# ScalarE's table sets, the grouping of its wide passes, and VectorE's instruction forms in a fused attention and rational-MLP kernel

## The chip, the cores and the metric

The kernel runs on one core of one Trainium2 chip. The metric is the device time of one execution in microseconds (us). Five things work side by side on the core: TensorE (PE in the profile; PEld is its weight load), VectorE (DVE), ScalarE (ACT), GpSimd (POOL), and the queue of the SyncE engine (SP), which issues the DMAs.

## What is computed

There are 4 batches of 12,480 rows of 128 numbers. Two attention steps through 32 inducing points (`h = mab(I, x)`, then `mab(x, h)`) give a matrix with one row for each row of x. It then goes through a two-layer network whose activation is a quotient of polynomials:

```
s = scale * (q @ kv^T);  a = softmax(s);  out = a @ kv
h = x @ w_in                           # 49920 x 2048
P = a0 + a1*h + a2*h^2 + a3*h^3
Q = 1 + |b0|*|h| + |b1|*h^2
y = (P / (Q + 1e-6)) @ w_out
```

## The kernel before

The network is nearly all of the time. A **unit** is one block of 480 rows by two slices of 128 of the 2048 hidden features, so a block has 8 units, a batch 26 blocks, and the kernel 832 units. `fast_ticks` (line 927) writes one unit into every engine's program per turn of its loop, a **tick** t, and the program order is kept as written. For unit u a tick holds:

- PE: two products into PSUM (`hp<-at,st`) and, 17 ticks later, the four passes of the second product (`po<-l,w_out`). For even units a further pair adds a shift (`hp<-same,by`).
- For even units DVE takes the absolute value of `hp` into SBUF (`row<-hp`, tensor_scalar). For odd units ACT does it (`row<-hp,all`, the function Abs).
- One tick later DVE forms a product from that value and `hp` (`l<-row,all,hp`, scalar_tensor_tensor), which also frees the PSUM buffer, of which there are three.
- ACT turns the absolute value into the reciprocal of the denominator in two steps, in place: a logarithm (Ln, `row<-row`) and a sigmoid (`row<-row,all`).
- 15 ticks after the unit, DVE (odd t, `l<-l,all,row`, called k3 below) and POOL (`row<-l,all`, then `l<-row`) form the last products for two units together.

Two neighbouring units are a **pair**, and a pair's values lie in one **room** of a ring of 9 rooms in SBUF. ACT handles Ln and sigmoid for 10 units (5 pairs, a **group**) together, so that it must load its function tables twice per group. `wide` (line 985) says in which of the group's ten turns which pairs are handled: Ln for pairs 0 and 1 at turn 0, 2 and 3 at turn 2, 4 at turn 4; sigmoid for pair 0 at turn 5, 1 and 2 at turn 6, 3 and 4 at turn 8. Two pairs in neighbouring rooms are one instruction of 128 x 3840. Where the ring wraps between them, they are two of 128 x 1920. ACT's Abs comes at every even turn, ahead of that turn's wide work.

The attention for later blocks and batches is spread between the units (`side`). It gives ACT exponentials: `e` for the first attention step (`exp_rows`) and `a` for the second (`pass3`). `run_act(turn == TURNS)` (line 974) lets them run at turn 5 only, that is, after a group's last Ln and ahead of its first sigmoid. The kernel loads the table set that has both Ln and Exp once, at its start; every later table load stands where the compiler put it, ahead of the first instruction whose function the loaded set lacks.

VectorE also has small work once per batch: `thirds` (line 623) splits a 128 x 128 matrix `gl` into three bf16 parts, `pass1` (line 376) reduces a row maximum (`mt`) and scales it (`nm`), and `bounded` (line 639) folds a flag `over` into a 32 x 1 column.

Of the kernel before, what the change touches and what calls it, by code (L numbers as in the profile page):

```python
# [9 lines left out]
F32 = mybir.dt.float32  # L10
# [6 lines left out]
ALU = mybir.AluOpType  # L17
PSUM = bass.MemoryType.PSUM

P = 128  # L20
TP = 120
M = 32
C = 128
# [8 lines left out]
TURNS = 5  # L32
# [159 lines left out]
class Kernel:  # L192
# [46 lines left out]
    def cast(self, engine, out, in_):  # L239
        engine.tensor_scalar(out=out, in0=in_, scalar1=1.0, scalar2=0.0, op0=ALU.mult, op1=ALU.add)  # L240
# [44 lines left out]
    def setup(self):  # L285
        nc, cp = self.nc, self.cp
        self.ind = cp.tile([C, M], F32, name="ind")
        nc.sync.dma_start(out=self.ind, in_=self.ind_c)
        self.ident = cp.tile([P, P], F32, name="ident")
        make_identity(self.tc.nc, self.ident)  # L290
        self.ones = cp.tile([1, 4], F32, name="ones")
        nc.vector.memset(self.ones, 1.0)
        self.fold = cp.tile([P, M], F32, name="fold")
        for j in range(4):
            rows = slice(M * j, M * j + M)
            nc.vector.tensor_copy(out=self.fold[rows], in_=self.ident[rows, rows])
        self.many = cp.tile([M, 4], F32, name="many")
        nc.vector.memset(self.many, 1.0)
        self.w_max = cp.tile([C, 8], F32, name="w_max")
        self.w_in = cp.tile([C, self.F], F32, name="w_in")  # L300
        self.w_out = cp.tile([P, self.NF, C], F32, name="w_out")
# [74 lines left out]
    def pass1(self, b):  # L376

        nc, ap = self.nc, self.ap
        X = mybir.AxisListType.X
        e = ap.tile([P, self.NG, BT], F32, tag="e", name=f"e{b}")  # L380
        mxs = ap.tile([P, self.NG, 2], F32, tag="mxs", name=f"mxs{b}")
        nc.gpsimd.memset(mxs, -3.0e38)
        xs = Blocks([], self.wide_columns(b), ahead=False) if self.boot else self.cols.pop((b, "a"))
        for g in range(self.NG):
            nb = min(4, self.NB - 4 * g)
            yield from self.landed("a", b, g)
            yield "pe", 1.0
            pc = self.misc(f"pc{b}_{g}")
            for j in range(nb):
                nc.tensor.matmul(pc[M * j:M * j + M, 0:BT], self.ind, xs.take(), start=True, stop=True)  # L390
                xs.read()
            rows = slice(0, M * nb)
            for i in range(2):
                yield "v", 0.36
                c = slice(BT // 2 * i, BT // 2 * (i + 1))
                nc.vector.tensor_scalar(out=e[rows, g, c], in0=pc[rows, c], scalar1=1.0, scalar2=None, op0=ALU.mult, op1=ALU.max, accum_out=mxs[rows, g, i:i + 1])
            self.free()
        if self.boot:
            self.wide_rows(b)
        else:  # L400
            self.xs[b] = [self.x_rows(b, n) for n in range(4)]
        yield "v", 0.1
        mx = ap.tile([P, 1], F32, tag="mx", name=f"mx{b}")
        nc.vector.tensor_reduce(out=mx, in_=mxs.rearrange("p g i -> p (g i)"), axis=X, op=ALU.max)
        yield "pe", 0.2
        pm = self.misc(f"pm{b}")
        nc.tensor.transpose(out=pm[0:1, 0:P], in_=mx, identity=self.ident)
        yield "v", 0.3
        mt = ap.tile([1, 1, M], F32, tag="mt", name=f"mt{b}")
        nc.vector.tensor_reduce(out=mt[:, 0], in_=pm[0:1, 0:P].rearrange("o (j m) -> o m j", m=M), axis=X, op=ALU.max)  # L410
        self.free()
        nm = ap.tile([1, 4, M], F32, tag="H", name=f"nm{b}")
        nc.vector.tensor_scalar(out=nm, in0=mt.broadcast_to((1, 4, M)), scalar1=-1.0 / math.sqrt(C), scalar2=None, op0=ALU.mult)
        yield "pe", 0.2
        pb = self.misc(f"pb{b}")
        nc.tensor.matmul(pb[:, 0:4], nm.rearrange("o j m -> o (j m)"), self.ones, start=True, stop=True)
        yield "v", 0.1
        nmc = ap.tile([P, 1], F32, tag="nmc", name=f"nmc{b}")
        nc.vector.tensor_copy(out=nmc, in_=pb[:, 0:1])
        self.free()  # L420
        self.e[b] = e
        self.exps.append(lambda: self.exp_rows(b, e, nmc))
        self.flush()
# [199 lines left out]
    def thirds(self, b, g):  # L623

        V, lin = self.nc.vector, self.lin[b]
        top, rest = slice(0, 2 * M), slice(2 * M, 4 * M)
        parts = g[:, 3 * C:4 * C].bitcast(BF16).rearrange("p (i d) -> p i d", d=C)
        hi, mid = parts[:, 0], parts[:, 1]
        x, y, z = (g[:, C * i:C * i + C] for i in range(3))
        self.cast(V, hi, x)  # L630
        V.tensor_tensor(out=y, in0=x, in1=hi, op=ALU.subtract)
        self.cast(V, mid, y)
        V.tensor_tensor(out=z, in0=y, in1=mid, op=ALU.subtract)
        self.cast(V, lin[top, 0:C], x[top])
        self.cast(V, lin[rest, 0:C], y[rest])
        self.cast(V, lin[top, C:], z[top])
        V.memset(lin[rest, C:], 0.0)

    def bounded(self, b):

        nc, ap, p = self.nc, self.ap, self.params
        if b == 0:
            for j in range(4):
                for i, op in ((j, ALU.max), (4 + j, ALU.min)):
                    yield "v", 0.6
                    nc.vector.tensor_reduce(out=self.w_max[:, i:i + 1], in_=self.w_in[:, 512 * j:512 * j + 512], axis=mybir.AxisListType.X, op=op)
            yield "v", 0.3
            nc.vector.scalar_tensor_tensor(out=self.w_max[:, 0:4], in0=self.w_max[:, 4:8], scalar=-1.0, in1=self.w_max[:, 0:4], op0=ALU.mult, op1=ALU.max)
            nc.vector.tensor_reduce(out=self.w_max[:, 4:5], in_=self.w_max[:, 0:4], axis=mybir.AxisListType.X, op=ALU.max)
        yield "v", 0.15  # L650
        mag = ap.tile([C, M], F32, tag="H", name=f"mag{b}")
        nc.vector.scalar_tensor_tensor(out=mag, in0=self.HT[b][:, 0:M], scalar=-1.0, in1=self.HT[b][:, 0:M], op0=ALU.mult, op1=ALU.max)
        yield "pe", 0.2
        pm = self.misc(f"bound{b}")
        nc.tensor.matmul(pm[0:M, 0:4], mag, self.w_max[:, 4:8], start=True, stop=True)
        yield "v", 0.3
        r = slice(0, M)
        over = ap.tile([M, 1], F32, tag="over", name=f"over{b}")
        nc.vector.tensor_scalar(out=over, in0=pm[r, 0:1], scalar1=p.mag_kappa[r], scalar2=p.room[r], op0=ALU.mult, op1=ALU.is_gt)
        self.free()  # L660
        nc.vector.tensor_tensor(out=p.bad[r], in0=p.bad[r], in1=over, op=ALU.max)
        if b == self.B - 1:
            yield "pe", 0.2
            pn = self.misc("redone")
            nc.tensor.matmul(pn[0:1, 0:4], p.bad[r], self.many, start=True, stop=True)
            yield "v", 0.2
            nc.vector.tensor_scalar(out=p.redo[0:1], in0=pn[0:1, 0:1], scalar1=0.5, scalar2=None, op0=ALU.is_gt)
            self.free()
# [258 lines left out]
    def fast_ticks(self, units):  # L927
# [4 lines left out]
        V, A, p = self.nc.vector, self.nc.scalar, self.params  # L932
        n = len(units)
# [7 lines left out]
        for t in range(n + BEHIND + 3):  # L941
            u, last, d, done = at(t), at(t - 1), at(t - BEHIND), at(t - BEHIND - 2)
            group, turn = divmod(t - TURNS - 2, 2 * TURNS)
            wide = self.wide(units, group, turn) if group >= 0 else None
# [27 lines left out]
            if u and plain(u):  # L972
                self.moved(u)
            self.run_act(turn == TURNS)
            for w in wide or ():
                if turn < TURNS:
                    A.activation(w, w, AF.Ln, bias=LAM, scale=LAM / Z)
                else:
                    A.activation(w, w, AF.Sigmoid, bias=p.lnc, scale=-2.0)
# [4 lines left out]

    def wide(self, units, group, turn):

        first = {0: (0, 2), 2: (2, 2), 4: (4, 1), TURNS: (0, 1), TURNS + 1: (1, 2), TURNS + 3: (3, 2)}
        k, n = first.get(turn, (0, 0))
        pairs = units[2 * (TURNS * group + k):2 * (TURNS * group + k + n):2]
        rows = []  # L990
        for u in pairs:
            r = self.at_room(u.n)
            if rows and rows[-1][1] == r:
                rows[-1][1] = r + 1
            else:
                rows.append([r, r + 1])
        return [self.row[:, lo:hi] for lo, hi in rows]
# [170 lines left out]
```

## Time and profile before

| what | value |
|---|---|
| runs | 2332.75, 2334.54, 2338.04 us; median 2334.54 |
| the profiled execution | 2333.67 us, span 2331.9 us |
| PE busy | 2153.3 us, 92% |
| VectorE busy | 2152.5 us, 92% |
| ScalarE busy | 2139.8 us, 92% |
| GpSimd busy | 1479.3 us, 63% |
| ScalarE's table loads | 195, 250.2 us in all |
| mean granted TensorE clock | 0.964 |

A share of busy time is a mean over the whole span; the first 7% of it (weights, the first batch's attention) has little to do with the rest. The rows below therefore also show busy times stretch by stretch. Idle time is a stretch's length less the busy time.

### The profile page before, as it was taken

The page shows a single profiled execution, that of the slowest core. Times are in us where ns is not written, and L with a number is a line of the kernel's source. Part 1 is how long each engine was busy: PE and PEld are TensorE (multiplying, and loading weights), DVE is VectorE, ACT ScalarE, POOL GpSimd, SP SyncE. Part 2 cuts the span into 40 slices and gives each one's busy share as a digit, 9 for nine tenths or more (in the row PEclk, how much of TensorE's full clock was granted, in tenths as well). Part 3 has the DMA queues.
Part 4 walks back from the last instruction along what each step waited for, and adds up shares of the span by engine and source line. Part 5 has one row for each costly group of instructions (what it writes and reads, how often), then busy time and mean ns, then how long its engine had stood idle before and what let it go on. Part 6 is the DMA issues. An engine that isn't in the chain of part 4 may idle for free.

```text
span 2331.9 us, 23875 instructions
## 1 busy us (share of the span) xinstructions
PE 2153.3 (92%) x7744; PEld 976.1 (42%) x7744; DVE 2152.5 (92%) x2372; ACT 2139.8 (92%) x1256; POOL 1479.3 (63%) x1039
## 2 busy tenths in 40 slices
PE   4378998999899999998999999989999999999997
PEld 2133444444344444444444444434444444444443
DVE  2788998999999999999999899999999999999995
ACT  1087999999899999998999999989999999999995
POOL 0234666676666666667666666776766676676666
PEclk7588999999999999999999999999999999999999
DMA  9302220131122101321231031001101100000000
GB/s 244 91 2 84 89 73 21 48 81 43 47 89 91 55 16 43 81 64 36 88 91 56 14 85 47 26 13 56 49 24 34 38 18 28 19 18 20 14 17 19
DMA packets 117103, 120.89 MB, mean 52 GB/s; under 512 B 13289, under 2 KB 115561, under 8 KB 116969
## 3 DMA queue, kind: packets, MB, share of 16 engines
q1 hardware_dynamic: 116969, 119.28, 17.7%
q8 instruction: 63, 1.03, 0.2%
q14 instruction: 71, 0.58, 0.1%
HBM read 80.89 MB, written 25.56 MB: 46 GB/s over the span
## 4 chain that ended last, share of the span: by engine, by line
PE 35%; ACT 27%; DVE 17%; issue 14%; DMA 2%; POOL 2%; SPq 1%; ACTq 0%; DVEq 0%; POOLq 0%
PE po L176 23%; ACT row L176 23%; PE hp L176 9%; DVE l L176 8%; DVE row L176 5%; ACT L176 4%; SPq L176 1%; DMA row<-x_c 1%; POOL l L176 1%; PE ph L176 1%; PE pc L176 1%; POOL row L176 1%; DMA raw<-w_in 1%; DVE gl L176 1%; PE pd L176 1%
## 5 line engine op out<-in xcount | busy, mean ns | idle before, releaser
L176 PE MATMUL po<-l,w_out 128*128 128x480 f32 x3328 | 1565.6, 576 | 6.4 <-POOL l L176 3.7
L176 DVE SCALAR_TENSOR_TENSOR l<-row,all,hp 128x960 f32<-128x960 f32 x832 | 1002.5, 1205 | 47.3 <-ACT row L176 36.3
L176 POOL TENSOR_TENSOR l<-row 128x960 f32<-128x960 f32 x416 | 930.3, 2236 | 34.6
L176 POOL TENSOR_SCALAR row<-l,all 128x960 f32<-128x960 f32 x416 | 445.4, 1071 | 697.2 <-DVE l L176 597.4
L176 PEld LDWEIGHTS po<-l,w_out 128*128 128x128 f32 x3328 | 620.1, 191 | 407.8 <-issue 239.6
L176 ACT ACTIVATE row<-row,all 128x3840 f32<-128x3840 f32 (+1 forms) x269 | 741.6, 2764 | 1.0
L176 ACT ACTIVATE row<-row 128x3840 f32<-128x3840 f32 (+1 forms) x268 | 717.4, 2683 | 6.5 <-DVE l L176 5.3
L176 DVE SCALAR_TENSOR_TENSOR l<-l,all,row 128x960 f32<-128x960 f32 x416 | 534.1, 1285 | 2.9 <-ACT row L176 2.9
L176 PE MATMUL hp<-at,st 128*128 128x480 f16 x1664 | 478.8, 370 | 47.3 <-DVE l L176 36.1
L176 DVE TENSOR_SCALAR row<-hp 128x960 int32<-128x960 int32 x416 | 476.9, 1146 | 10.9 <-PE hp L176 10.2
L176 ACT ACTIVATE row<-hp,all 128x960 f32<-128x960 f32 x416 | 436.5, 1049 | 47.9 <-PE hp L176 42.2
L176 PEld LDWEIGHTS <-st 128*128 128x128 f16 x1872 | 182.1, 98 | 533.7 <-issue 513.3
L176 PE MATMUL hp<-same,by 96*128 96x480 f16 x832 | 240.0, 369 | 35.8 <-DVE row L176 29.1
L176 ACT ACT_TABLE_LOAD x195 | 250.2, 1283 | 4.0 <-PEq L1161 0.7
L176 PEld LDWEIGHTS <-by 96*128 96x128 f16 x832 | 82.0, 99 | 227.9 <-issue 201.1
L176 DVE COPY oT<-po 128x480 f32<-128x480 f32 x104 | 67.9, 653 | 47.4 <-PE po L176 46.9
L176 PE MATMUL po<-at,st 128*128 128x480 f16 x208 | 60.0, 370 | 2.9 <-DVE st L176 2.9
L176 ACT ACTIVATE a<-a 120x512 f32<-120x512 f32 (+2 forms) x21 | 14.9, 727 | 35.7 <-DVE a L176 35.6
L176 ACT ACTIVATE e<-e,nmc 128x960 f32<-128x960 f32 (+1 forms) x16 | 15.6, 993 | 31.9 <-DVE nmc L176 31.7
L176 DVE TENSOR_SCALAR_CACHE_REDUCE e<-pc 128x240 f32<-128x240 f32 (+1 forms) x56 | 20.8, 402 | 24.8 <-PE pc L176 24.8
L176 POOL TENSOR_TENSOR row<-row 128x384 f32<-128x384 f32 (+2 forms) x11 | 11.8, 1075 | 43.2 <-DVE row L176 36.9
L176 POOL TENSOR_TENSOR a<-a,asm 120x512 f32<-120x512 f32 (+1 forms) x27 | 36.8, 1363 | 1.7 <-PE bound L176 1.7
(119 smaller groups left out, 599.0 us busy)
## 6 DMA issues: line engine op xcount, KB each, us to landing
xTb<-x_c SPq DMA_DIRECT2D x104, 240.0 KB, 3.3
out<-oT SPq DMA_DIRECT2D x104, 240.0 KB, 2.0
xTa<-x_c SPq DMA_DIRECT2D x78, 240.0 KB, 3.2
x<-x_t SPq DMA_DIRECT2D x78, 240.0 KB, 4.1
at<-hl SPq DMA_DIRECT2D x416, 30.0 KB, 1.8
row<-x_t SPq DMA_DIRECT2D x8, 720.0 KB, 14.2
row<-x_c SPq DMA_DIRECT2D x5, 960.0 KB, 12.3
raw<-w_in SPq DMA_DIRECT2D x4, 480.0 KB, 11.3
```

The costliest lines, as they stand in the source:

```text
L176: ins = call(*args, **kw)
```

## The change

Four edits:

- At turn 0 of each group the kernel itself asks for the table set that has both Ln and Exp (`preload_act_table_set`), ahead of the Ln instructions.
- `wide` has two timetables for Ln and two for sigmoid, and takes the one whose twos of pairs don't lie across the end of the ring (`cut` is the number of pairs up to it). It also returns nothing behind the last group.
- In `thirds` and `bounded`, tensor_scalar and tensor_tensor become scalar_tensor_tensor (times 1.0, then the operation; a cast is x*1 max x).
- In `pass1` the scaling instruction `nm` goes: the reduction writes its result four times, and the factor moves into the constant `ones` of the product behind it.

```diff
-        nc.vector.memset(self.ones, 1.0)
+        nc.vector.memset(self.ones, -1.0 / math.sqrt(C))
...
-        mt = ap.tile([1, 1, M], F32, tag="mt", name=f"mt{b}")
-        nc.vector.tensor_reduce(out=mt[:, 0], in_=pm[0:1, 0:P].rearrange("o (j m) -> o m j", m=M), axis=X, op=ALU.max)
+        mt = ap.tile([1, 4, M], F32, tag="H", name=f"mt{b}")
+        nc.vector.tensor_reduce(out=mt, in_=pm[0:1, 0:P].rearrange("o (a j m) -> o a m j", a=1, m=M).broadcast_to((1, 4, M, 4)), axis=X, op=ALU.max)
         self.free()
-        nm = ap.tile([1, 4, M], F32, tag="H", name=f"nm{b}")
-        nc.vector.tensor_scalar(out=nm, in0=mt.broadcast_to((1, 4, M)), scalar1=-1.0 / math.sqrt(C), scalar2=None, op0=ALU.mult)
...
-        self.cast(V, hi, x)
-        V.tensor_tensor(out=y, in0=x, in1=hi, op=ALU.subtract)
...
+        def cast(out, in_):
+            V.scalar_tensor_tensor(out=out, in0=in_, scalar=1.0, in1=in_, op0=ALU.mult, op1=ALU.max)
+
+        cast(hi, x)
+        V.scalar_tensor_tensor(out=y, in0=x, scalar=1.0, in1=hi, op0=ALU.mult, op1=ALU.subtract)
...
-        nc.vector.tensor_tensor(out=p.bad[r], in0=p.bad[r], in1=over, op=ALU.max)
+        nc.vector.scalar_tensor_tensor(out=p.bad[r], in0=p.bad[r], scalar=1.0, in1=over, op0=ALU.mult, op1=ALU.max)
...
             self.run_act(turn == TURNS)
+            if turn == 0 and wide:
+                A.preload_act_table_set("natural_log_exp_and_others")
             for w in wide or ():
...
-        first = {0: (0, 2), 2: (2, 2), 4: (4, 1), TURNS: (0, 1), TURNS + 1: (1, 2), TURNS + 3: (3, 2)}
-        k, n = first.get(turn, (0, 0))
+        if 2 * TURNS * group >= len(units):
+            return []
+        cut = -units[2 * TURNS * group].n % self.rooms["u"]
+        logs = {0: (0, 1), 2: (1, 2), 4: (3, 2)} if cut in (1, 3) else {0: (0, 2), 2: (2, 2), 4: (4, 1)}
+        sigs = {0: (0, 2), 2: (2, 2), 4: (4, 1)} if cut in (2, 4) else {0: (0, 1), 1: (1, 2), 3: (3, 2)}
+        k, n = (logs if turn < TURNS else sigs).get(turn % TURNS, (0, 0))
```

How it moves instructions, at two places. The first is ScalarE in batch 0, from the table load of one group to the sigmoid of its first pair; `a_2` is an exponential of the second attention step. Before:

```order
L176 ACT_TABLE_LOAD
L176 ACTIVATE row<-row 128x3840
L176 ACTIVATE row<-hp_4_7_1271,all 128x960
L176 ACTIVATE row<-row 128x1920 x2
L176 ACTIVATE row<-hp_5_1_1296,all 128x960
L176 ACTIVATE row<-row 128x1920
L176 ACT_TABLE_LOAD
L176 ACTIVATE a_2_1140<-a_2_1140 120x512
L176 ACT_TABLE_LOAD
L176 ACTIVATE row<-row,all 128x1920
```

And ScalarE at the same place in the changed kernel:

```order
L176 ACT_TABLE_LOAD
L176 ACTIVATE row<-row 128x1920
L176 ACTIVATE row<-hp_4_7_1272,all 128x960
L176 ACTIVATE row<-row 128x3840
L176 ACTIVATE row<-hp_5_1_1296,all 128x960
L176 ACTIVATE row<-row 128x3840
L176 ACTIVATE a_2_1140<-a_2_1140 120x512
L176 ACT_TABLE_LOAD
L176 ACTIVATE row<-row,all 128x1920
```

The load between the last Ln and the exponential is gone, the two halves at the ring's end are one instruction, and the single pair now comes first instead of last. Over the whole fast path there are 26 table loads fewer (27 gone, one new at the first group), and of 37 places with two halves in a row one is left. The group that starts with the first sigmoid in the last row is moved in the same way where its cut is 2 or 4.

The second place is VectorE in batch 0, where `thirds` prepares batch 1's matrix. Before:

```order
L176 SCALAR_TENSOR_TENSOR gl_3652<-prep_3637,base 128x128
L176 TENSOR_SCALAR gl_3652<-gl_3652 128x128
L176 TENSOR_TENSOR gl_3652<-gl_3652 128x128
L176 TENSOR_SCALAR gl_3652<-gl_3652 128x128
L176 TENSOR_TENSOR gl_3652<-gl_3652 128x128
L176 TENSOR_SCALAR st_3375<-gl_3652 64x128 x3
```

And VectorE there in the changed kernel:

```order
L176 SCALAR_TENSOR_TENSOR gl_3658<-prep_3643,base 128x128
L176 SCALAR_TENSOR_TENSOR gl_3658<-gl_3658 128x128 x4
L176 SCALAR_TENSOR_TENSOR st_3380<-gl_3658 64x128 x3
```

The same seven steps stand at the same place; only their form changed. The instructions of GpSimd, of the DMA queue and of TensorE keep their order.

## Rows read from the trace of the kernel before

**Rows 1.** Busy us (instructions) by stretch: PE, PEld, DVE, ACT, POOL; clock, DMA

```profile
181.00:338.00 157.00, 147.81 (x508) 64.41 (x506) 150.47 (x179) 142.43 (x83) 95.04 (x65) 0.96 0.28 84
572.00:770.00 198.00, 187.27 (x629) 82.40 (x628) 195.53 (x221) 182.96 (x102) 132.02 (x90) 0.97 0.22 69
1043.00:1270.00 227.00, 219.61 (x754) 97.61 (x752) 225.52 (x255) 216.62 (x124) 154.95 (x105) 0.98 0.23 71
1510.00:1640.00 130.00, 122.65 (x384) 54.91 (x383) 127.85 (x131) 120.62 (x69) 92.70 (x60) 0.97 0.10 33
338.00:572.00 234.00, 224.67 (x918) 105.54 (x919) 216.38 (x219) 231.41 (x141) 155.13 (x118) 0.98 0.18 48
770.00:1043.00 273.00, 264.65 (x1064) 123.59 (x1063) 258.15 (x260) 272.29 (x166) 181.09 (x136) 0.99 0.18 51
1270.00:1510.00 240.00, 232.33 (x944) 108.84 (x944) 225.69 (x227) 238.71 (x144) 157.76 (x121) 0.99 0.17 45
1640.00:2290.00 650.00, 631.15 (x1991) 284.39 (x1990) 629.53 (x592) 648.39 (x365) 442.02 (x276) 1.00 0.08 25
```

**Rows 2.** Timeline around an exponential (start, duration in us, engine; idle before, releaser)

```profile
1299.88 1.80 ACT L176 ACTIVATE row<-row 128x1920 f32<-128x1920 f32 x1
...
1301.69 1.28 ACT L176 ACT_TABLE_LOAD   x1
...
1302.99 1.10 ACT L176 ACTIVATE e<-e,nmc 128x960 f32<-128x960 f32 x1
...
1306.34 1.90 ACT L176 ACTIVATE row<-row,all 128x1920 f32<-128x1920 f32 x1
...
1309.22 1.22 DVE L176 SCALAR_TENSOR_TENSOR l<-row,all,hp 128x960 f32<-128x960 f32 x1 [2.41 <-ACT row L176]
```

**Rows 3.** ScalarE's groups by shape: count, busy us, mean ns

```profile
L176 ACT ACT_TABLE_LOAD x195 | 250.2, 1283 | 4.0 <-PEq L1161 0.7
L176 ACT ACTIVATE row<-row 128x3840 f32<-128x3840 f32 x148 | 503.3, 3400 | 3.1 <-DVE l L176 2.1
```

**Rows 4.** Timeline of ScalarE: one wide sigmoid, one in halves, and the first Ln

```profile
670.82 3.48 ACT L176 ACTIVATE row<-row,all 128x3840 f32<-128x3840 f32 x1
...
675.15 3.67 ACT L176 ACTIVATE row<-row,all 128x1920 f32<-128x1920 f32 x2
...
130.64 3.40 ACT L176 ACTIVATE row<-row 128x3840 f32<-128x3840 f32 x1
```

**Rows 5.** Timeline of VectorE and GpSimd: k3 beside GpSimd's product, in batch 0

```profile
397.40 2.23 POOL L176 TENSOR_TENSOR l<-row 128x960 f32<-128x960 f32 x1
...
398.60 2.05 DVE L176 SCALAR_TENSOR_TENSOR l<-l,all,row 128x960 f32<-128x960 f32 x1
...
1297.47 1.21 DVE L176 SCALAR_TENSOR_TENSOR l<-l,all,row 128x960 f32<-128x960 f32 x1
```

**Rows 6.** Timeline of VectorE and GpSimd: the split of `gl` in batch 0

```profile
613.92 0.28 DVE L176 SCALAR_TENSOR_TENSOR gl<-prep,base 128x128 f32<-128x128 f32 x1
614.23 0.24 DVE L176 TENSOR_SCALAR gl<-gl 128x128 bf16<-128x128 f32 x1
614.48 2.23 POOL L176 TENSOR_TENSOR l<-row 128x960 f32<-128x960 f32 x1
614.51 2.35 DVE L176 TENSOR_TENSOR gl<-gl 128x128 f32<-128x128 f32 x1
```

**Rows 7.** Timeline of VectorE: `mt` and `nm`; below, a reduction of 512 elements, grouped

```profile
333.68 0.27 DVE L176 TENSOR_REDUCE mt<-pm 1x32 f32<-1x128 f32 x1
333.99 2.22 DVE L176 TENSOR_SCALAR nm<-mt 1x128 f32<-1x128 f32 x1
...
L176 DVE TENSOR_REDUCE amx<-ps 120x16 f32<-120x512 f32 x24 | 16.4, 685 | 1.9 <-PE ps L176 1.9
```

**Rows 8.** Timeline of ScalarE and VectorE: an Abs and the product that reads it

```profile
689.87 1.06 ACT L176 ACTIVATE row<-hp,all 128x960 f32<-128x960 f32 x1 [0.79 <-PE hp L176]
...
694.73 1.20 DVE L176 SCALAR_TENSOR_TENSOR l<-row,all,hp 128x960 f32<-128x960 f32 x1
```

More of the change, by code (lines that the diff above doesn't have):

```diff
@@ L408, in pass1 @@
         yield "v", 0.3
-        mt = ap.tile([1, 1, M], F32, tag="mt", name=f"mt{b}")
-        nc.vector.tensor_reduce(out=mt[:, 0], in_=pm[0:1, 0:P].rearrange("o (j m) -> o m j", m=M), axis=X, op=ALU.max)
+        mt = ap.tile([1, 4, M], F32, tag="H", name=f"mt{b}")
+        nc.vector.tensor_reduce(out=mt, in_=pm[0:1, 0:P].rearrange("o (a j m) -> o a m j", a=1, m=M).broadcast_to((1, 4, M, 4)), axis=X, op=ALU.max)
         self.free()
-        nm = ap.tile([1, 4, M], F32, tag="H", name=f"nm{b}")
-        nc.vector.tensor_scalar(out=nm, in0=mt.broadcast_to((1, 4, M)), scalar1=-1.0 / math.sqrt(C), scalar2=None, op0=ALU.mult)
         yield "pe", 0.2
         pb = self.misc(f"pb{b}")
-        nc.tensor.matmul(pb[:, 0:4], nm.rearrange("o j m -> o (j m)"), self.ones, start=True, stop=True)
+        nc.tensor.matmul(pb[:, 0:4], mt.rearrange("o j m -> o (j m)"), self.ones, start=True, stop=True)
         yield "v", 0.1
@@ L629, in thirds @@
         x, y, z = (g[:, C * i:C * i + C] for i in range(3))
-        self.cast(V, hi, x)
-        V.tensor_tensor(out=y, in0=x, in1=hi, op=ALU.subtract)
[L632 to L636, printed above, removed]
+        def cast(out, in_):
+            V.scalar_tensor_tensor(out=out, in0=in_, scalar=1.0, in1=in_, op0=ALU.mult, op1=ALU.max)
+        cast(hi, x)
+        V.scalar_tensor_tensor(out=y, in0=x, scalar=1.0, in1=hi, op0=ALU.mult, op1=ALU.subtract)
+        cast(mid, y)
+        V.scalar_tensor_tensor(out=z, in0=y, scalar=1.0, in1=mid, op0=ALU.mult, op1=ALU.subtract)
+        cast(lin[top, 0:C], x[top])
+        cast(lin[rest, 0:C], y[rest])
+        cast(lin[top, C:], z[top])
         V.memset(lin[rest, C:], 0.0)
```

## The prediction

> **What bounds the kernel now.** I read busy time by stretch first, because the page's 92% for each of three engines decides nothing. Rows of the view fall into two kinds [rows 1]. In the four stretches from 338, 770, 1270 and 1640 us, 1397 us in all, ScalarE is busy 231.4 + 272.3 + 238.7 + 648.4 = 1390.8 us, so it idles for 6 us, while VectorE idles for 67 us (1397 less 216.4 + 258.2 + 225.7 + 629.5). There ScalarE sets the pace. In the other four, 712 us in all, VectorE idles for 13 us and ScalarE for 49: there VectorE does. What a shorter ScalarE program is worth must be read from the first kind, and what a shorter VectorE program is worth from the second. TensorE idles for 44 us in the first kind, so it stands close behind both.
>
> Next I read the timeline where an exponential runs [rows 2]. The last Ln ends at 1301.68, a table load of 1.28 us follows at once, then two exponentials, a second load and, at 1306.34, the sigmoid, and behind that the next Abs. VectorE has waited 2.41 us for that Abs when it goes on at 1309.22. So the loads lie on the path there. The first of the two is the one that goes.
>
> **The change part by part.** The sum is made against the profiled execution, 2333.7 us; the median of the runs, 2334.5, is 0.8 above it.
>
> *Table loads.* The trace has 195 [rows 3]. The order of the changed kernel has 27 fewer and one new. A load costs its 1.283 us and, beyond that, an overlap: two neighbouring sigmoids of 1.90 us each [rows 2] are together 3.67 and not 3.80 [rows 4], so ACTIVATEs overlap by some 0.1 us, while a load starts only when the instruction ahead has ended, and the next only when the load has [rows 2]. So 1.38 us each. By their place in the trace, 17 of the 27 lie in the stretches that ScalarE bounds (5, 5, 4 and 3). 17 x 1.38 = 23.5 us, all of it on the path, because ScalarE has no idle time there and VectorE has 67 us to take the gain from.
>
> *Halves.* A wide sigmoid takes 3.48 us, one in two halves 3.67 [rows 4], so 0.19 us per place. Of the 37 places, 24 lie in those stretches: 4.6 us. Together with the loads, 28.1.
>
> *The same two edits where VectorE bounds.* Ten loads and eleven halves would be 10 x 1.38 + 11 x 0.19 = 15.9 us of ScalarE. VectorE covers them. The gain lies between 0 and VectorE's 12.6 us of idle time, and since that is only 1.8% of these stretches, against 4.8% in the others, I take 1.5.
>
> *The new load in the first group.* 1.4 us on ScalarE, which starts that group's first Ln at 130.64 us [rows 4] and is the late one there. Between 0 and 1.4; I take 1.4, a loss.
>
> *Does Ln cost the same from the shared set?* Until the first sigmoid, the kernel before still has the set loaded that it asked for at its start. Its first Ln, at 130.64 us, took 3.40 us [rows 4], as the mean of all [rows 3]. So nothing is lost there.
>
> *`nm` and `mt`.* The scaling goes. In the row shown it took 2.22 us behind a reduction of 0.27 [rows 7]; another of the four took 2.29, the other two 0.21. The reduction now reads 512 elements instead of 128; the nearest row, 512 elements per partition on 120 partitions, takes 0.685 [rows 7]. So two places go from 2.5 to 0.7 us and a third loses 0.2 (the fourth is in the start). Both long ones are at 334 and 760 us, where VectorE bounds: 3.7 - 0.2, a gain of 3.5.
>
> *The three-operand form.* What makes the small work long is not its length. The tensor_tensor on `gl` at 614.51 us lasts 2.35 us, to 616.86, just beyond the end (616.71) of a GpSimd product that began 0.03 us before it; a cast just ahead took 0.24 and a scalar_tensor_tensor that reads PSUM 0.28 [rows 6]. Eight instructions of `thirds` and `bounded` were held up in that way, by some 12 us in all. Does the new form escape? The trace has one of this form with both inputs in SBUF, k3. Started at 398.60 us inside a GpSimd product that ended at 399.63, it lasted 2.05 us, to 1.02 behind that end; free, it lasts 1.21 [rows 5]. It was held up too. I take the hold-ups to stay: 0. What is left is the cast, 0.28 against 0.24, seven per batch: a loss of about 1 us over four batches. The bounds are -12 (all escape) and +3 (the seven are also held up where they were not).
>
> The Trainium skill ("SBUF — State Buffer", section "Who interferes with whom") speaks against this edit: a VectorE instruction with two SBUF inputs shares a read interface with GpSimd instructions that read SBUF, and whichever comes second waits for the whole of the first. It puts tensor_tensor and every other form with two SBUF inputs on one footing. By that rule this edit is worth 0. By the one free row of 0.28 it would be worth the 12 us.
>
> *Sum.* -28.1 - 1.5 + 1.4 - 3.5 + 1.0 = -30.7, so 2333.7 - 30.7 = **2303**. Late next, once ScalarE is 28 us shorter, is VectorE: its 67 us of idle time in ScalarE's stretches fall to about 39.
>
> **The rivals.**
>
> *VectorE takes over sooner.* Its 67 us are not all slack: part is waiting for TensorE or for GpSimd, and k3 is held up more often as VectorE draws level. For it: the longest stretch that ScalarE bounds, of 650 us, holds only 20 us of VectorE's idle time [rows 1]. Against it: the wait of 2.41 us just behind an exponential [rows 2]. If half of the 28 is lost, the time is 2317.
>
> *The new form escapes GpSimd.* For it: the free 0.28 of a scalar_tensor_tensor [rows 6]. Against it: k3 [rows 5]. 12 us more, since nearly all of it lies where VectorE bounds: 2291.
>
> *A longer run between two Abs, and slower.* Where the cut is 1 to 4, the new timetables put two pairs in one instruction beside the change of tables: a Ln of 3.40 in place of 1.80, or a sigmoid of 3.48 in place of 1.90, between the Abs of turn 4 and that of turn 6. This run grows by 1.6 us in 37 groups. If each is a wait of VectorE, that is 59 us, and the time is 2333.7 + 59 - 30.7 = 2362. What decides is ScalarE's lead over VectorE. Where VectorE bounds, an Abs ended at 690.93 and was read at 694.73, a lead of 3.8 us [rows 8], which covers 1.6. Where ScalarE bounds, the lead is nothing [rows 2], but the other runs of that group become shorter by the same amount, and a ScalarE that never idles loses nothing by a different order. The rival wins if TensorE, held up with VectorE, can't keep ScalarE fed afterwards; with 44 us of idle time in 1397 it has little to make up with.
>
> *A change of tables costs more than the load's own bar.* Then each load gone is worth more. In the trace the load starts 0.01 us behind the Ln and the exponential 0.02 behind the load [rows 2], so I give it 1 in 100. With a further 1.4 us of ScalarE, about a load's own length, for each of the 17, the time would be 2303 - 24 = 2279. The Trainium skill ("ScalarE: Activation LUTs", section "What ACT_TABLE_LOAD costs") has such a price, 1283 ns and a drain of 1380 ns, 2.66 us in all; by it the loads would bring 45 us instead of 23.5. The trace shows the first figure and no drain.
>
> *The change doesn't do what it says.* The new order shows the loads gone, and the explicit load where the implicit one stood. Nothing is left of this but that something unseen eats the gain: 2 in 100.
>
> **How the numbers follow.** The forecast has 0.58, VectorE's taking over 0.22, the escape 0.12, the slower case 0.05, the drain 0.01, no effect 0.02. The forecast alone, with its bounds of 1.5 to 12.6 for ScalarE's work under VectorE, 0 to 1.4 for the new load and a few microseconds of shifted hold-ups, reaches from 2293 to 2313. The range has to take in most of the escape (2291) and of the take-over (2317): 2286 to 2321. About 0.2%, 4.7 us, can be told from no change. Faster by more than that are all cases but the slower one and no effect, and the slower one, met halfway, may come out even: 0.93 faster, 0.03 the same, 0.04 slower.
>
> **What the profile after would show.** Right: 169 table loads; no load between a Ln and an exponential; VectorE's wait behind it about 1 us instead of 2.4; ScalarE's busy time down by about 42 us (26 x 1.38 + 36 x 0.19), VectorE's idle time in ScalarE's stretches down to about 39 us; tensor instructions on `gl` that still last about 2 us beside a GpSimd product. Wrong: the `gl` steps all at 0.3 us (the escape); ScalarE idle for 20 us or more in the stretches it bounds now (take-over); VectorE waiting for Abs in groups whose cut is 1 to 4, by 1.6 us more than in the others, with ScalarE idle behind it (slower).

## The result and the profile after

The changed kernel takes 2312.16 us (median; 2310.33 to 2313.14), the kernel before, run beside it on the same chip, 2333.64. The ratio is 0.9904, with a 95% interval of 0.9887 to 0.9921. The profiled execution took 2313.14 us, with a span of 2311.3. So the change makes the kernel faster by about 21 us, where 31 were forecast. The time lies in the forecast range, and 9 us above the forecast.

The page of the changed kernel, its busy times and its groups (columns as in [rows 3]; the third part is the idle time just before the group and what ended most of it):

```profile
PE 2146.0 (93%) x7744; PEld 975.0 (42%) x7744; DVE 2147.9 (93%) x2368; ACT 2101.0 (91%) x1193; POOL 1483.0 (64%) x1039
...
L176 DVE SCALAR_TENSOR_TENSOR l<-row,all,hp 128x960 f32<-128x960 f32 x832 | 999.5, 1202 | 32.4 <-ACT row L176 23.7
...
L176 PE MATMUL hp<-at,st 128*128 128x480 f16 x1664 | 477.2, 369 | 42.8 <-DVE l L176 32.9
L176 ACT ACTIVATE row<-hp,all 128x960 f32<-128x960 f32 x416 | 436.7, 1050 | 62.2 <-PE hp L176 61.3
...
L176 ACT ACT_TABLE_LOAD x169 | 216.8, 1283 | 3.5 <-PEq L1168 0.7
```

Two of these groups in the kernel before:

```profile
L176 DVE SCALAR_TENSOR_TENSOR l<-row,all,hp 128x960 f32<-128x960 f32 x832 | 1002.5, 1205 | 47.3 <-ACT row L176 36.3
...
L176 ACT ACTIVATE row<-hp,all 128x960 f32<-128x960 f32 x416 | 436.5, 1049 | 47.9 <-PE hp L176 42.2
```

Table loads fell from the 195 of [rows 3] to 169, as forecast, at the same 1283 ns each. ScalarE is busy 38.8 us less than before (2139.8 less 2101.0). But the kernel gained only 20.6 us of span, so ScalarE now idles more. What it waits for is the fourth row: ahead of an Abs it waits 62.2 us in all, 61.3 of them for TensorE, against 47.9 and 42.2 before.

Where the time went is read stretch by stretch, as in [rows 1]. The eight stretches below hold the same instructions as those of [rows 1]: each boundary is moved by as much as the copy `oT<-po` of the nearest block of 8 units moved. The view of the changed kernel (busy us by stretch: PE, PEld, DVE, ACT, POOL; clock, DMA):

```profile
182.65:337.92 155.27, 147.57 (x506) 64.37 (x504) 148.75 (x178) 135.22 (x76) 95.07 (x65) 0.95 0.27 85
337.92:567.07 229.15, 223.35 (x919) 105.14 (x919) 217.04 (x219) 225.32 (x134) 155.27 (x118) 0.99 0.18 49
567.07:761.79 194.72, 185.50 (x629) 81.67 (x628) 193.36 (x220) 178.82 (x96) 131.34 (x90) 0.98 0.23 70
761.79:1030.16 268.37, 262.21 (x1064) 123.02 (x1063) 258.30 (x261) 266.17 (x157) 183.03 (x137) 1.00 0.19 52
1030.16:1257.62 227.46, 220.14 (x754) 97.73 (x752) 225.93 (x254) 214.16 (x117) 155.12 (x105) 0.98 0.23 70
1257.62:1492.06 234.44, 230.98 (x944) 108.33 (x944) 225.35 (x227) 231.62 (x136) 157.06 (x121) 1.00 0.17 46
1492.06:1621.80 129.74, 122.19 (x384) 54.91 (x383) 128.00 (x131) 120.19 (x66) 92.62 (x60) 0.97 0.10 33
1621.80:2268.51 646.71, 630.17 (x1991) 284.82 (x1990) 629.55 (x592) 642.10 (x351) 444.42 (x276) 0.99 0.08 25
```

The four stretches that ScalarE bounds (second, fourth, sixth, eighth) were 1397 us long and are 1378.7: a gain of 18.3. In them ScalarE is busy for 1365.2 us instead of 1390.8, and idles for 13.5 instead of 6.2. The other four were 712 us and are 707.2: a gain of 4.8. The part ahead of the first stretch grew by 1.65 us and the part behind the last by 0.9. That makes -18.3 - 4.8 + 1.65 + 0.9 = -20.6, the difference of the two spans.

The place of [rows 2] in the changed kernel. The timeline has ScalarE's last Ln, two exponentials without a load between, the one load that is left and the sigmoid, and VectorE's product behind the next Abs:

```profile
1283.27 3.40 ACT L176 ACTIVATE row<-row 128x3840 f32<-128x3840 f32 x1 [0.36 <-DVE l L176]
1286.58 1.08 ACT L176 ACTIVATE e<-e,nmc 128x960 f32<-128x960 f32 x1
1287.56 1.04 ACT L176 ACTIVATE a<-a 120x1024 f32<-120x1024 f32 x1
1288.62 1.28 ACT L176 ACT_TABLE_LOAD   x1
1289.92 1.90 ACT L176 ACTIVATE row<-row,all 128x1920 f32<-128x1920 f32 x1
...
1292.79 1.21 DVE L176 SCALAR_TENSOR_TENSOR l<-row,all,hp 128x960 f32<-128x960 f32 x1 [0.50 <-ACT row L176]
```

VectorE's wait here fell from the 2.41 us of [rows 2] to 0.50, although the last Ln is now the wide one. It is 0.13 in the kernel with the same loads and the old timetable (below).

### The profile page after: what moved, and what is told of

Same layout as the page of the kernel before. It is cut to its first block, busy times and chain, and to the rows that moved or that the text cites. A ratio compares the mean times of both kernels' runs of the same rounds, so it can differ in the third digit from the quotient of the medians.

```text
span 2311.3 us, 23789 instructions
## 1 busy us (share of the span) xinstructions
PE 2146.0 (93%) x7744; PEld 975.0 (42%) x7744; DVE 2147.9 (93%) x2368; ACT 2101.0 (91%) x1193; POOL 1483.0 (64%) x1039
## 4 chain that ended last, share of the span: by engine, by line
PE 47%; DVE 20%; ACT 16%; issue 12%; POOL 2%; DMA 2%; SPq 1%; DVEq 0%; POOLq 0%; ACTq 0%
PE po L176 31%; ACT row L176 13%; PE hp L176 12%; DVE l L176 10%; DVE row L176 6%; ACT L176 2%; SPq L176 1%; PE ph L176 1%; DMA row<-x_c 1%; POOL l L176 1%; PE pd L176 1%; PE pc L176 1%; POOL row L176 1%; DVE gl L176 1%; DVE oT L176 1%
## 5 line engine op out<-in xcount | busy, mean ns | idle before, releaser
L176 DVE SCALAR_TENSOR_TENSOR l<-row,all,hp 128x960 f32<-128x960 f32 x832 | 999.5, 1202 | 32.4 <-ACT row L176 23.7
L176 POOL TENSOR_SCALAR row<-l,all 128x960 f32<-128x960 f32 x416 | 448.1, 1077 | 673.8 <-DVE l L176 603.8
L176 ACT ACTIVATE row<-row,all 128x3840 f32<-128x3840 f32 (+1 forms) x250 | 738.1, 2953 | 1.0
L176 ACT ACTIVATE row<-row 128x3840 f32<-128x3840 f32 (+1 forms) x250 | 715.9, 2864 | 8.0 <-DVE l L176 6.8
L176 DVE SCALAR_TENSOR_TENSOR l<-l,all,row 128x960 f32<-128x960 f32 x416 | 533.3, 1283 | 4.6 <-ACT row L176 4.6
L176 PE MATMUL hp<-at,st 128*128 128x480 f16 x1664 | 477.2, 369 | 42.8 <-DVE l L176 32.9
L176 ACT ACTIVATE row<-hp,all 128x960 f32<-128x960 f32 x416 | 436.7, 1050 | 62.2 <-PE hp L176 61.3
L176 ACT ACT_TABLE_LOAD x169 | 216.8, 1283 | 3.5 <-PEq L1168 0.7
L176 DVE TENSOR_SCALAR_CACHE_REDUCE e<-pc 128x240 f32<-128x240 f32 (+1 forms) x56 | 20.6, 397 | 24.4 <-PE pc L176 24.4
L176 POOL TENSOR_TENSOR row<-row 128x384 f32<-128x384 f32 (+2 forms) x11 | 11.9, 1085 | 42.8 <-DVE row L176 35.3
```

What stands on the lines that cost most here:

```text
L176: ins = call(*args, **kw)
```

## The experiments

The four edits were taken one by one first. My theory was the prediction's: the loads carry the gain, halves add a little, the three-operand form nothing. The rival after the result was that the new timetables of `wide`, and not some overlap of the gains, took away what is missing. Every kernel ran beside the kernel before on the same chip. The traces of two kernels agree block by block wherever nothing changed: of the 103 blocks of two kernels below that differ in the three-operand form alone, 94 are equal to 0.02 us. So I also give a difference "by blocks": the time from the first to the last copy `oT<-po`. It leaves out the kernel's start, since the first copy comes between 179.2 and 183.8 us in the twelve traces. It is taken from one execution of each kernel, so it has no spread of its own. By blocks the change gains 22.0 us.

**The table loads alone.**

```diff
             self.run_act(turn == TURNS)
+            if turn == 0 and wide:
+                A.preload_act_table_set("natural_log_exp_and_others")
```

> Only the explicit table load is kept; the timetables, the small VectorE work and the scaling are those of the kernel before. Theory A (the new timetables give back what they save): the 26 loads alone bring nearly all that is left of the change once the scaling is taken off, 18 to 24 us. Rival B (VectorE takes over sooner, as the prediction's rival says, and the timetables are worth their 0.19 us per place): the loads bring 11 to 15 us. By the prediction's own sum: 17 x 1.38 + 1.5 - 1.4 = 23.6 us.

Measured: 2310.05 us (2308.37 to 2313.58), ratio 0.9906 [0.9891, 0.9922]; 24.0 us gained by blocks. This one edit gives all that the whole change gives, and by blocks 2 us more.

**The timetables alone.** `wide` as in the changed kernel, all else as before.

```diff
-        first = {0: (0, 2), 2: (2, 2), 4: (4, 1), TURNS: (0, 1), TURNS + 1: (1, 2), TURNS + 3: (3, 2)}
...
+        logs = {0: (0, 1), 2: (1, 2), 4: (3, 2)} if cut in (1, 3) else {0: (0, 2), 2: (2, 2), 4: (4, 1)}
+        sigs = {0: (0, 2), 2: (2, 2), 4: (4, 1)} if cut in (2, 4) else {0: (0, 1), 1: (1, 2), 3: (3, 2)}
```

> Only the grouping of wide passes is changed. Theory A: even or slower, 0 to +5 us: in groups whose cut is 1 to 4 VectorE waits about 2.5 us for the Abs behind the longer run, TensorE waits with it and is slow afterwards, and ScalarE then idles 0.6 to 1.4 us. Rival B: 4 to 5 us faster (24 places x 0.19 us), with no more idle time of ScalarE.

Measured: 2338.79 us (2335.21 to 2344.17, 10 runs), ratio 1.0024 [1.0014, 1.0035]; 6.6 us lost by blocks. So this edit makes the kernel slower, by a little more than the 0 to 5 us expected. Its group of VectorE products:

```profile
L176 DVE SCALAR_TENSOR_TENSOR l<-row,all,hp 128x960 f32<-128x960 f32 x832 | 1000.1, 1202 | 57.3 <-ACT row L176 47.8 <-PE hp L176 9.0
```

VectorE waits 57.3 us ahead of this product, against 47.3 in the kernel before (36.3 of it for ScalarE). With the boundaries moved as above, the four stretches that VectorE bounds are 5.4 us longer and the four that ScalarE bounds 0.8. In the first four VectorE had not waited for ScalarE ahead of this product at all; now it waits some 5.3 us there. So the lead of 3.8 us at one place [rows 8] did not cover 1.6 at every place.

**`mt` and `nm` alone.** The edit of `pass1` and of `ones`, as in the diff of the change.

> Only the scaling instruction and the reduction ahead of it are changed. From the two blocks of the trace that became shorter around it (1.9 and 3.6 us): 5 to 6 us faster, about 0.2%. By the prediction's sum: 3.5 us. If those two blocks became shorter through the loads instead: under 1 us.

Measured: 2330.53 us, ratio 0.9991 [0.9982, 1.0001]; 3.2 us gained by blocks. By the times alone this can't be told from nothing, and the 5 to 6 us that I had expected did not come; the prediction's 3.5 is nearer. The trace shows the edit: the reduction that stands in place of both instructions takes 0.67 us in each of the four batches.

```profile
L176 DVE TENSOR_REDUCE mt<-pm x4: 671/672/679, 31.0 to 1225.8; 1x128 f32<-1x512 f32 x4
```

**The three-operand form alone.** The edits of `thirds` and `bounded`.

> Only the form of the instructions in thirds and bounded is changed. If the new form is held up by GpSimd as the old one is: within 1.5 us of the kernel before, and single steps on gl that last 2 us. If it escapes: 9 to 12 us faster, every step on gl at 0.3 us.

Measured: 2334.1 us, ratio 1.0004 [0.9996, 1.0013]; 0.26 us lost by blocks. The eight casts and eight subtractions in the view of the tile `gl` (shortest, median and longest, in ns):

```profile
L176 DVE SCALAR_TENSOR_TENSOR gl<-gl x16: 279/535/2290, 176.5 to 1541.0; 128x128 bf16<-128x128 f32 x8, 128x128 f32<-128x128 f32 x8
```

The longest still lasts 2.29 us: it starts at 614.08, 0.09 us behind the start of a GpSimd product, and ends 0.15 us behind that product's end. The new form is held up beside GpSimd as the old one was.

**Loads and `pass1` together**, with the old timetable and the old forms.

> The explicit load and the shorter scaling, with the timetables and the forms of the kernel before. Theory A (the four edits add up, and the timetables are a loss): 22.9 + 2.4 = 25 us below the kernel before, some 2307 to 2309 us, faster than the changed kernel and than the loads alone. Rival (the changed kernel's loss is not the timetables but the edits hiding each other): 2310 to 2313, no better than the loads alone.

Measured: 2305.69 us (2303.31 to 2308.55), ratio 0.9885 [0.987, 0.99]; 29.1 us gained by blocks, 7.1 more than by the whole change. A part of the change does better than the change.

**The sigmoids' timetable, and the logarithms', each on top of those two.** In each only one of the two lines above was put in.

> As the first of these four, with the new timetable for the sigmoid alone (groups whose cut is 2 or 4). Theory A (the long run between two Abs is the loss, worst where an exponential falls into it): 1 to 4 us slower than the first of these four, VectorE waiting some 2.5 us behind the load in these groups. Rival (the loss comes from the Ln timetable): level with it, or 1 us faster.

> The loads and the pass1 edit (2305.7 us measured) plus the new Ln timetable alone (cut 1 and 3). Theory (a longer run between two Abs holds up TensorE wherever an exponential or ScalarE-bound stretch follows): a loss of 2 to 4 us against 2305.7, 2307.5 to 2309.5, in the trace as block losses of 0.4 to 1.1 us near 360, 805 to 870, 1285, 1700 and 1820 us, with VectorE's idle time up by as much and TensorE's too, and nothing in the stretches that VectorE bounds. Rival (halves saved count where ScalarE bounds, as forecast): a gain of 2 to 3 us, 2303. Rival (the remaining loss of the changed kernel comes from the three-operand form): no change here, 2305 to 2306.5.

Measured: 2307.43 us (2303.35 to 2315.0) and 2307.12 (2305.43 to 2312.49), against 2305.69 for the two edits alone. By the times neither can be told from it. By blocks they lose 1.9 and 1.6 us, at places: the sigmoids' in the last batch (+1.6 and +1.1 us in two neighbouring blocks, 1.8 of it given back in the two after), the logarithms' near 360, 801 and 822 us (+0.4, +0.7, +1.0). In the stretches that VectorE bounds the logarithms' lose 0.55 us in one block. The sigmoids' lose 0.8 us in one block there and gain 1.8 in another, at 1077 us, where the flag's product in `bounded` happened to miss GpSimd: it took 0.15 us, against 2.23 with the two edits alone. Without that gain they would have lost 3.7. For the logarithms I had expected 2 to 4 us; they cost a little less.

**The changed kernel with the old timetable.**

> The changed kernel with the old timetable of the wide passes: loads, pass1 edit and three-operand form. Theory (the form costs about 0.3 us in each of three later batches and the timetable alone explains the rest): 2305.5 to 2307.5, that is 5 to 6 us faster than the changed kernel's 2312.2. Rival (the form matters beside the loads, since VectorE is nearer to bounding): 2308 or more.

Measured: 2305.68 us (2303.44 to 2310.16), ratio 0.9891 [0.9875, 0.9908]. The medians are 6.5 us below the changed kernel's, as expected, though the two intervals overlap. By blocks the difference is 6.6 us, and 0.5 from loads and `pass1` alone, of which 0.28 and 0.30 stand in the blocks where batches 1 and 2 split `gl`. So the new timetable takes away some 6.6 us, more than its two halves one by one (3.5, or 5.4 without the gain at 1077 us). The four stretches that ScalarE bounds, in this kernel:

```profile
334.58:563.28 228.70, 223.35 (x919) 104.99 (x919) 217.11 (x219) 226.74 (x138) 155.45 (x119) 0.99 0.18 49
...
757.96:1024.66 266.70, 262.37 (x1064) 123.03 (x1063) 258.75 (x261) 265.73 (x161) 183.09 (x137) 1.00 0.19 52
...
1252.10:1486.23 234.13, 230.98 (x944) 108.34 (x944) 225.41 (x227) 232.62 (x141) 157.15 (x121) 1.00 0.17 46
...
1615.54:2259.79 644.25, 629.17 (x1991) 283.72 (x1990) 629.56 (x592) 642.74 (x362) 444.52 (x276) 1.00 0.08 25
```

They last 1373.8 us, with 1367.8 of ScalarE: 6.0 idle, as much as before. With the new timetable ScalarE has 2.6 us less to do in them (1365.2) and idles 7.5 us more (13.5), so they are 4.9 us longer. In the first three, which hold 2.4 of the 4.9, TensorE's granted clock is the same with both timetables (0.99, 1.00, 1.00). With the old timetable the groups of waits are shorter too:

```profile
L176 DVE SCALAR_TENSOR_TENSOR l<-row,all,hp 128x960 f32<-128x960 f32 x832 | 999.8, 1202 | 26.4 <-ACT row L176 18.7 <-PE hp L176 6.9
L176 PE MATMUL hp<-at,st 128*128 128x480 f16 x1664 | 477.2, 369 | 36.8 <-DVE l L176 26.9 <-DMA at<-hl 5.5 <-POOL st L176 1.5
L176 ACT ACTIVATE row<-hp,all 128x960 f32<-128x960 f32 x416 | 436.5, 1049 | 54.8 <-PE hp L176 47.2 <-POOL l L176 7.0
```

**How one place loses.** In the last batch a group begins its sigmoids with two pairs in the changed kernel and with one in the kernel with the old timetable. First the changed kernel's timeline (ScalarE from the load on, VectorE's product, TensorE), then its busy times (as in [rows 1]) from 2050.0 and 2055.7 us:

```profile
2048.71 1.28 ACT L176 ACT_TABLE_LOAD   x1
2050.00 3.50 ACT L176 ACTIVATE row<-row,all 128x3840 f32<-128x3840 f32 x1
2053.41 1.05 ACT L176 ACTIVATE row<-hp,all 128x960 f32<-128x960 f32 x1
...
2061.20 1.06 ACT L176 ACTIVATE row<-hp,all 128x960 f32<-128x960 f32 x1 [0.63 <-PE hp L176]
...
2054.49 1.21 DVE L176 SCALAR_TENSOR_TENSOR l<-row,all,hp 128x960 f32<-128x960 f32 x1 [2.58 <-ACT row L176]
...
2055.75 0.56 PE L176 MATMUL hp<-at,st 128*128 128x480 f16 x2 [2.68 <-DVE l L176]
2056.32 4.38 PE L176 MATMUL po<-l,w_out 128*128 128x480 f32 x6
```

```profile
2050.00:2055.70 5.70, 3.07 (x11) 1.19 (x10) 3.12 (x4) 5.70 (x3) 3.12 (x2) 1.00 0.01 3
2055.70:2061.00 5.30, 5.25 (x11) 2.09 (x11) 5.30 (x6) 4.87 (x3) 3.30 (x2) 0.68 0.12 46
```

And the same place with the old timetable, timeline and busy times:

```profile
2042.25 1.90 ACT L176 ACTIVATE row<-row,all 128x1920 f32<-128x1920 f32 x1
2044.06 1.04 ACT L176 ACTIVATE row<-hp,all 128x960 f32<-128x960 f32 x1
...
2045.13 1.22 DVE L176 SCALAR_TENSOR_TENSOR l<-row,all,hp 128x960 f32<-128x960 f32 x1 [0.98 <-ACT row L176]
...
2046.40 0.57 PE L176 MATMUL hp<-at,st 128*128 128x480 f16 x2 [1.08 <-DVE l L176]
2046.96 2.68 PE L176 MATMUL po<-l,w_out 128*128 128x480 f32 x6
```

```profile
2046.30:2051.50 5.20, 5.10 (x15) 2.30 (x15) 5.20 (x7) 5.20 (x4) 3.21 (x2) 1.00 0.12 47
```

Behind the load stands a sigmoid of 3.50 us instead of 1.90. VectorE waits 2.58 us for the Abs instead of 0.98: the 1.6 us of the prediction's slower rival. TensorE waits 2.68 instead of 1.08. After that wait the granted clock of the next 5.3 us is 0.68, a mean between the levels 1.2 and 2.4 GHz, and six passes of the second product take 4.38 us; with the old timetable the clock stays at 1.00 and the same six take 2.68. With TensorE late by a further 1.7 us, ScalarE then waits 0.63 us for its next `hp`.

The wait by itself did not bring the clock down. The kernel with the timetables alone has the same wait at the same place (TensorE's timeline, then the busy times behind it):

```profile
2082.88 0.57 PE L176 MATMUL hp<-at,st 128*128 128x480 f16 x2 [2.68 <-DVE l L176]
2083.45 2.68 PE L176 MATMUL po<-l,w_out 128*128 128x480 f32 x6
```

```profile
2082.90:2088.20 5.30, 5.30 (x16) 2.38 (x16) 5.30 (x6) 5.30 (x4) 3.31 (x2) 1.00 0.13 46
```

There the clock stays at 1.00, the six passes take 2.68 us, and ScalarE does not wait for the `hp` behind them. Over the four blocks from this place on, the new timetable costs 0.6 us in the kernel where the clock fell (+1.6, +1.1, -1.2, -0.8) and gains 0.6 in the one where it did not (+1.6, -0.3, -1.3, -0.6). By the difference the slower clock cost about 1.2 us here. Why it fell in one kernel and not in the other stays open.

In the changed kernel VectorE has such a wait (2.47, 2.58, 2.59 us) at 1929, 2054 and 2153 us, where the kernel with the old timetable has 0.87, 0.98 and 0.97. The slower clock follows the last two. Behind the first, TensorE waits only 1.18 us and its clock stays at 1.00, and the block is 1.4 us longer all the same. In its other groups no such wait is longer than 1.28 us, but for one of 3.02 in the first group, which both kernels have. ScalarE's 0.63 us behind each of the two slow places is 1.3 of the 7.5 us that it idles more. The rest lies elsewhere, in waits for TensorE or VectorE that no run ties one by one to a longer instruction.

**The small work with its operands in PSUM.** If operands in SBUF are what exposes `gl`, then keeping the matrix and its remainders in the PSUM tile `prep` should end the hold-ups, in the old two-operand form. The subtractions then have one input in SBUF and the casts none. The step ahead of them writes `prep` too, and `prep` is given back only behind them. In the kernel before, the steps take (view of the tile `gl`):

```profile
L176 DVE TENSOR_SCALAR gl<-gl x8: 218/733/1150, 177.2 to 1539.8; 128x128 bf16<-128x128 f32 x8
L176 DVE TENSOR_TENSOR gl<-gl x8: 291/452/2345, 177.4 to 1540.9; 128x128 f32<-128x128 f32 x8
```

Not only the subtractions were held up: four of the casts, which have one input in SBUF, lasted 1.04 to 1.15 us beside a GpSimd instruction, and so did `nm`, with one input, for 2.22 [rows 7]. The edit:

```diff
-        x, y, z = (g[:, C * i:C * i + C] for i in range(3))
+        x, y, z = (pr[:, C * i:C * i + C] for i in range(3))
...
-        over = ap.tile([M, 1], F32, tag="over", name=f"over{b}")
+        over = pm[r, 4:5]
```

> The kernel before, but thirds keeps its matrix and both remainders in PSUM, so that no instruction on them has two inputs in SBUF, and bounded does the same with its flag. Theory A (the hold-up comes from the second SBUF input, whatever the form): every step lasts 0.2 to 0.4 us, TensorE's idle time at the three places falls from about 5 us each, and the kernel is 8 to 15 us faster. Rival (the small steps are slow for another reason, or VectorE's stall is covered there): steps of 2 us remain, or the time is within 2 us of the kernel before.

Measured: 2326.81 us (2318.58 to 2328.7, 8 runs), ratio 0.9967 [0.9955, 0.9978]. The steps, in the view of the tile `prep`:

```profile
L176 DVE TENSOR_SCALAR gl<-prep x8: 291/292/292, 174.7 to 1542.7; 128x128 bf16<-128x128 f32 x8
L176 DVE TENSOR_TENSOR prep<-prep,gl x8: 299/299/300, 175.1 to 1543.0; 128x128 f32<-128x128 f32 x8
```

None lasts longer than 0.30 us, where the same work took up to 2.35 [rows 6], and six of each eight ran beside a GpSimd instruction. The gain is 5.7 us, below the 8 to 15 expected.

**Loads, `pass1` and PSUM operands together.**

> The explicit load, the shorter scaling and the small work in PSUM together. If the gains add: 25 us and what the run above brings, 2292 to 2300 us, faster than every other version. If they hide each other: 2303 to 2308.

Measured: 2292.39 us (2291.29 to 2294.0), ratio 0.9826 [0.9813, 0.984]. It beats the kernel before by 40 us and the changed kernel by 20. On top of loads and `pass1` the PSUM operands bring 13.3 us. A part of that again goes through TensorE's clock. With loads and `pass1` only, TensorE's timeline behind the split of batch 1, and the busy times around it:

```profile
613.72 0.96 PE L176 MATMUL hp<-same,by 96*128 96x480 f16 x2 [4.52 <-DVE row L176]
```

```profile
609.00:613.50 4.50, 0.20 (x1) 0.00 (x0) 4.32 (x8) 4.37 (x3) 2.23 (x2) 0.82 0.00 0
613.50:618.00 4.50, 4.12 (x8) 1.55 (x8) 4.50 (x7) 0.00 (x0) 1.23 (x2) 0.50 0.38 116
```

With PSUM operands TensorE waits 2.63 us there, and the 5 us after it have a mean clock of 0.68, not 0.50:

```profile
604.10 0.96 PE L176 MATMUL hp<-at,st 128*128 128x480 f16 x2 [2.63 <-DVE l L176]
```

```profile
604.00:609.00 5.00, 4.91 (x13) 2.08 (x13) 4.97 (x8) 4.41 (x3) 3.68 (x4) 0.68 0.00 0
```

Behind the split of batch 2 the wait is 2.63 us as well (at 1079.80), and there the 5 us after it have a clock of 1.00.

Why the same edit brought 5.7 us alone and 13.3 beside the other two is answered in part. By blocks (5.1 and 13.2 us) two blocks differ by 8.1 us together; the other differences cancel. The block at 1226 us is 5.3 us longer with the edit alone and unchanged beside the other two; the one at 443 us is 4.1 and 1.3 us longer. In the first, with the edit alone, stands an `nm` that is now held up, where it took 0.21 us in the kernel before; the edit of `pass1` removes it:

```profile
1239.37 2.28 DVE L176 TENSOR_SCALAR nm<-mt 1x128 f32<-1x128 f32 x1
```

The second stays open. Alone, the edit's runs spread over 10 us.

## Why the prediction was right in part, point by point

| term | forecast, us | measured, us |
|---|---|---|
| loads, where ScalarE bounds | -23.5 | -23.2 (four stretches, old timetable, `pass1` with them; -22.4 for the loads alone) |
| halves and the new order there | -4.6 | +4.9 (1378.7 less 1373.8) |
| the other four stretches: ScalarE's work, `nm`, form | -1.5 - 3.5 + 1.0 = -4.0 | -4.8 |
| start (the new load) | +1.4 | +1.65, not told from its spread |
| the end, behind the last stretch | 0 | +0.9 |
| sum | -30.7 | -20.6 |

- **Loads: right.** The edit alone gives 4.3, 6.4, 5.9 and 5.8 us in the four stretches, 22.4 in all for 17 loads: 1.32 us each, against 1.38 taken. It gives 1.5 in the other four, as taken. The row of -23.2 is 1397 less the 1373.8 us of the changed kernel with the old timetable. That a drain comes on top of each load, the Trainium skill's 2.66 us ("ScalarE: Activation LUTs", section "What ACT_TABLE_LOAD costs"), would by an estimate from that figure have shown as about 45 us in these stretches; it is not there.
- **VectorE's cover: right.** In the stretches that VectorE bounds, ScalarE's busy time falls by 14.2 us in the changed kernel (662.6 to 648.4), and most of it becomes idle time. VectorE's idle time in ScalarE's stretches fell to 48.4 us, where 39 were forecast, and to 42.9 with the old timetable. So the rival that VectorE takes over sooner is not what happened.
- **`nm` and `mt`: right.** A gain of 3.5 was forecast; the edit alone gained 3.2 by blocks, and 5.1 on top of the loads (29.1 less 24.0).
- **The form: right.** 1.0 us of loss was forecast, 0.26 by blocks measured for the edit alone, and no hold-up went. The rule of the Trainium skill ("SBUF — State Buffer", section "Who interferes with whom") gave 0 for it, and the trace agrees: 2.28 us is the longest `gl` step in the changed kernel, 2.29 with this edit alone. The remedy that the rule points to, one input that is not in SBUF, took every subtraction to 0.30. Of the casts the prediction read only the free one of 0.24 [rows 6]; four of the eight lasted over 1 us in the same trace.
- **Halves: wrong, and this is the step that failed.** A gain of 4.6 was forecast and a loss of 4.9 measured. The size was off: the 0.19 us per place is a sigmoid's. By the groups' busy time a sigmoid's place saved 0.18 us (741.6 to 738.1 for 19) and a logarithm's 0.09 (717.5 to 715.9 for 18); in these stretches ScalarE has 2.6 us less to do. (None of the 37 places is left in the trace, where one was thought to remain.) What failed above all is the argument by which the slower rival was given only 5 in 100: "the other runs of that group become shorter by the same amount, and a ScalarE that never idles loses nothing by a different order". The order did cost. VectorE's waits ahead of its product grew from 26.4 to 32.4 us, TensorE's ahead of `hp<-at,st` from 36.8 to 42.8, and ScalarE idles 7.5 us more in these stretches. The prediction named this condition ("TensorE, held up with VectorE, can't keep ScalarE fed afterwards") and held it unlikely. It came in part: the wait of 1.6 us more at three places and smaller ones elsewhere, not in all 37 groups. A fallen clock made two of the three dearer. That the timetable costs the time is shown by the kernels with and without it; how each wait becomes lost time is shown at one place.
- **Luck in the range.** The time lies in it although a term has the wrong sign. The upper end, 2321, was drawn for the take-over, which did not happen. The slower rival as priced, 2362, lay outside; it came at a fraction of that price.
- **The end.** The 0.9 us behind the last stretch had no term. TensorE waits 1.98 us at 2280.99 there, and the next 5.3 us have a clock of 0.68; with the old timetable it waits 1.55 at 2271.84 and the clock stays at 1.00.
- **What was to be seen.** No load stands between a Ln and an exponential; at the place of [rows 2] the wait behind it is 0.50 us, better than the 1 us forecast. ScalarE's busy time fell by 38.8 us, not 42. ScalarE idles for 13.5 us in the stretches it bounded, between the 6 of the forecast and the 20 named for the take-over. The sign named for the slower case, a wait longer by 1.6 us with ScalarE idle behind it, is there at two places.

## What to carry to other kernels

Price an instruction that is taken away where its engine sets the pace: 17 loads of that kind gave nearly what they should (22.4 us of 23.5), ten others 1.5 us. Be slower to credit a reordering that makes fewer, longer instructions: look at the longest run between two results that another engine waits for, and where the run grows beyond that engine's lead, count its wait and the wait of the engine behind it, and allow for a slower clock after that. And when an instruction is held up by another engine's access, change where its operands lie; here a different instruction form with the same operands stayed held up.

## What the runs showed of the hardware

A wait of TensorE could cost more than its length. After waits of 4.52 and 2.68 us the next 4.5 and 5.3 us had granted clocks of 0.50 and 0.68 (0.50 is the level of 1.2 GHz), after one of 1.08 us the clock stayed at 1.00. With 0.68, six passes took 4.38 us in place of 2.68. The length of the wait does not decide it alone: after 2.68 us at the same place in another kernel, and after 2.63 in a third, the clock stayed at 1.00.

A VectorE subtraction with one operand in PSUM and one in SBUF ran in 0.30 us in all eight cases, six of them beside a GpSimd instruction. With both in SBUF, of the same size, it took 0.29 to 2.35 us. A cast took 0.29 us in all eight cases with its operand in PSUM, and 0.22 to 1.15 with it in SBUF.
